# Two-stage attention and a squared-ReLU MLP on one core: batch 0 cut by head sets and token parts, hand-placed PSUM banks and a new step order

## The chip, the cores and the metric

The kernel runs on one core of a Trainium2 chip. The metric is device time in microseconds (us). Before the change it is 250.41 us, the median of 3 runs (250.41 to 251.27).

Engines are named as in the profile: PE (TensorE matmuls) and PEld (its weight loads), DVE (VectorE), ACT (ScalarE), POOL (GpSimd, which here mostly issues the loads), SP (SyncE, which issues the stores and the DMA transposes). Every engine takes its own instructions in program order.

## The reference

```
q, k, v: 8 batches x 8 heads x 576 tokens x 64     p: 8 x 8 x 32 x 64
packed = softmax(p k^T / 8) v            # 32 packed rows per head
att    = softmax(q packed^T / 8) packed  # 576 rows per head, 64 wide
x      = att with the heads side by side # 4608 x 512
h = x @ w_in                             # 512 x 2048
g = s * relu(h)^2 + b
out = g @ w_out                          # 2048 x 512, float32
```

## The kernel before

The work goes batch by batch. The attention output x is never formed: the softmax weights of the second attention (aT, 256 packed rows by 576 tokens) multiply a product of the packed rows with w_in (pw), which gives h directly. In h, 128 of the 2048 hidden columns make one "m"; there are 16. The term b is added as b times the column sums of w_out (biasrep), and s when a result leaves PSUM (svec).

The order of all work is one list of words at the end of the kernel, run in sequence; each word emits the instructions of one step, and so sets the order within each engine. The letters are followed by batch and part numbers:

- **L..** loads on POOL's queue: Lk, Lq, Lv (batch, half of the heads), Lp and Lpall (p), Lwi and Lwo (quarters of w_in and w_out, 512 KB each as bf16), Lsb (s and b, on SP). The loads cast float32 to bf16.
- **T** (on_pe) turns k or q on PE and copies them out of PSUM, **D** does it by a DMA transpose for batches 2 to 7; **V** (order_v) re-orders v on DVE; **PD, PP, PA, PPA** double and turn p.
- **F** first scores and their exp, **P** the packed rows, **X** their transpose, **S** second scores and exp, **A** the softmax sums: a matmul with ones, Ln and Exp of the negative on ACT, and a product on DVE (**G** in batch 0) that gives aT.
- **W** (packed_w) multiplies packed rows with w_in. It works in 64x32 tiles of the PE, eight of them at a time, two quarters of 512 columns in one word (one in batch 0), and is evicted by ACT and DVE.
- **M** (mlp_in) is one m: four matmuls of 288 columns into a tile of two PSUM banks, a relu on ACT (on DVE for a few of batch 0), a square on DVE into gT. **h** (mlp_in_half) does it for two m and one half of the tokens, in batch 0.
- **O**b.t**x**n are n of the 16 matmuls of 512 columns that give output tile t of batch b; with the last of them DVE scales and adds the bias into ysb and SP stores it.
- **BT** sums the columns of w_out (it needs all of w_out); **BC** makes the sum equal on all partitions by two float32 matmuls.
- **Z** and **Y** are matmuls on a tile of zeros that nobody reads (zps, or the next hps tile).

PSUM has 8 banks: pool psh has two tiles of two banks (hps), pool psy four tiles of one bank, and a step waits until a tile of its pool is free. Of the loaded k, q and v there is one buffer each.

Of the kernel before, what the change touches and what calls it, by code (L numbers as in the profile page):

```python
# [14 lines left out]
def kernel(  # L15
# [32 lines left out]
    JJ = NP // 16  # L48

# [8 lines left out]
    psh = ctx.enter_context(tc.tile_pool(name="psh", bufs=2, space=bass.MemoryType.PSUM))  # L58
    psy = ctx.enter_context(tc.tile_pool(name="psy", bufs=4, space=bass.MemoryType.PSUM))
# [17 lines left out]
    early = []  # L77

    def big(dt=F32):
        if early:  # L80
            return early.pop()
        return psh.tile([P, 2, NB if dt == F32 else 2 * NB], dt, tag="h", name="hps")
# [12 lines left out]
    pn = [constp.tile([P, 2, 2, D], BF16, name=f"pn{i}") for i in range(2)]  # L95
    pall = constp.tile([16 * (B - 2), 16, 2, D], BF16, name="pall")
# [10 lines left out]
    rowsf = constp.tile([P, P], F32, name="rowsf")  # L107
# [7 lines left out]
    def load(what, b, h0=0, h1=H):  # L115
        src = {"k": k, "q": q, "v": v}[what]
        if h0 == 0:
            raw[what, b] = rawp.tile([R, H, NC * D], BF16, tag=what + "n", name=what + "n")
        pool.dma_start(
            out=raw[what, b][:, h0:h1, :],  # L120
            in_=src[b, h0:h1].rearrange("h (r c) d -> r h (c d)", c=NC),
        )

# [21 lines left out]
    def load_sb():  # L145
        sp.dma_start(out=svec[:], in_=moe_s[0:1].unsqueeze(0).to_broadcast([P, 1]))
        sp.dma_start(out=bvec[:], in_=moe_b[0:1].unsqueeze(0).to_broadcast([P, 1]))
# [6 lines left out]

    def prep_p(b):
        pt = big(BF16)
        for x in range(2):
            tr(
                pt[:, 0, x * P:(x + 1) * P],
                pn[b][:, x, :, :],  # L160
                identb[:],
            )
        for c2 in range(2):
            act.copy(
                out=pbd[D * c2:D * c2 + D, :, b, :, c2, :],
                in_=pt[D * c2:D * c2 + D, 0, 0:2 * P].rearrange("p (g a j) -> p a g j", g=4, a=2),
            )

    def prep_pall():
        n = 16 * (B - 2)  # L170
        pts = [psy.tile([P, 8 * P], BF16, tag="y", name="pps") for _ in range(2)]
# [6 lines left out]
        for x in range(2):  # L178
            src = pts[x][:].rearrange("p (t n) -> p t n", n=P)[:, :, 0:n].rearrange(
# [9 lines left out]
    def on_pe(b, what, half):  # L189
        dst = (kT if what == "k" else qT)[b % 2]  # L190
        if what == "q":
            dst = dst[:].rearrange("p h c r -> p (h c r)")
        tpw = big(BF16)
        tp = [tpw[:, 0], tpw[:, 1]]
        split = b == 0 and what == "q"
        if split:
            tp[1] = psy.tile([P, 2 * NB], BF16, tag="y", name="tps")
        for h4 in range(4):
            for cp in range(CP):
                o = (h4 % 2) * HS + cp * R  # L200
                tr(
                    tp[h4 // 2][:, o:o + R],
                    raw[what, b][:, 4 * half + h4, cp * P:(cp + 1) * P],
                    identb[0:R, 0:R],
                )
        d = dst[:, half * 4 * HS:(half + 1) * 4 * HS].rearrange("p (a s) -> p a s", a=2)
        if split:
            act.copy(out=d[:, 0], in_=tp[0][:, 0:2 * HS])
            vec.tensor_copy(out=d[:, 1], in_=tp[1][:, 0:2 * HS])
        else:  # L210
            vec.tensor_copy(out=d, in_=tpw[:, :, 0:2 * HS])
# [8 lines left out]
    def order_v(b, h0=0, h1=H):  # L220
        vec.tensor_copy(
            out=vr[:, :, h0:h1, 0:D].rearrange("r c h d -> r h c d"),
            in_=raw["v", b][:, h0:h1, :].rearrange("r h (c d) -> r h c d", c=NC),
        )

    def first_scores(b, a):
        if a == 0:
            e1[b] = attp.tile([R, 2, NC, 4, NP], BF16, tag="e1", name="e1")
        s1 = big()
        for g in range(4):  # L230
            for cp in range(CP):
# [8 lines left out]
                )  # L240
        act.activation(
# [8 lines left out]
    def packed(b, half=None):  # L250

        if not half:
            pps[b] = psy.tile([P, NB], F32, tag="y", name="pps")
        pp = pps[b][:, 0:2 * DV].rearrange("p (a x) -> p a x", a=2)
        for a in range(2):
            for c in range(NC):
                for g in range(4) if half is None else (2 * half, 2 * half + 1):
# [8 lines left out]
        if half == 0:  # L266
            return
        rd = smp.tile([P, 2], F32, tag="rd", name="rd")
        vec.reciprocal(out=rd[:], in_=pp[:, :, D])
        pk[b] = smp.tile([P, 2, 2, D], BF16, tag="pk", name="pk")  # L270
        for a in range(2):
# [6 lines left out]
    def turned(b):  # L278

        pt = pps[b][:, NB // 2:].bitcast(BF16)  # L280
        for a in range(2):
            tr(pt[:, a * P:(a + 1) * P], pk[b][:, a].rearrange("p c d -> p (c d)"), identb[:])
        vec.tensor_copy(
            out=ppd[b % 2][:].rearrange("p a g j -> p (a g j)"),
            in_=pt[:, 0:2 * P],
        )

    def second_scores(b, by_half=False, with_w=False):
        e2[b] = attp.tile([P, 2, S], BF16, tag="e2", name="e2")
        tiles = [big() for _ in range(2)]  # L290
        for a in range(2):
            for g in range(4):
                for c2 in range(2):
                    t, i = (c2, a) if by_half else (a, c2)
                    mm(
                        tiles[t][NP * g:NP * g + NP, i, 0:HS],
# [6 lines left out]
        if by_half:  # L303
            exp_half(b, tiles, 0, 0)
            exp_half(b, tiles, 1, 0)
            s2[b] = tiles
            return
        if with_w:
            packed_w(b, [0])
        for a in range(2):  # L310
            act.activation(
# [6 lines left out]
    def exp_half(b, tiles, a, hf):  # L318
        act.activation(
            out=e2[b][:, a, hf * HS:(hf + 1) * HS],  # L320
            in_=tiles[hf][:, a, 0:HS],
            func=AF.Exp,
            scale=scale,
        )

    def weights_half(b, hf):
        if hf == 0:
            aT[b] = atp.tile([P, 2, S], BF16, tag="aT", name="aT")
        dps = big()
        for a in range(2):  # L330
            mm(dps[:, a, 0:HS], onesbd[:], e2[b][:, a, hf * HS:(hf + 1) * HS], start=True, stop=True)
        if hf == 0:
            exp_half(b, s2[b], 0, 1)
            exp_half(b, s2[b], 1, 1)
        ld = smp.tile([P, 2, HS], F32, tag="ld", name="ld")
        act.activation(out=ld[:], in_=dps[:, :, 0:HS], func=AF.Ln)
        rcd[hf] = smp.tile([P, 2, HS], F32, tag="rcd", name="rcd")
        act.activation(out=rcd[hf][:], in_=ld[:], func=AF.Exp, scale=-1.0)

    def weigh_half(b, hf):  # L340
        cols = slice(hf * HS, (hf + 1) * HS)
        vec.tensor_tensor(out=aT[b][:, :, cols], in0=e2[b][:, :, cols], in1=rcd[hf][:], op=ALU.mult)

    def weights(b, a):
        if a == 0:
            aT[b] = atp.tile([P, 2, S], BF16, tag="aT", name="aT")
        dps = big()
        for hf in range(2):
            mm(dps[:, hf, 0:HS], onesbd[:], e2[b][:, a, hf * HS:(hf + 1) * HS], start=True, stop=True)
        ld = smp.tile([P, 2, HS], F32, tag="ld", name="ld")  # L350
        act.activation(out=ld[:], in_=dps[:, :, 0:HS], func=AF.Ln)
        rc = smp.tile([P, S], F32, tag="rcd", name="rcd")
        act.activation(out=rc[:], in_=ld[:].rearrange("p a s -> p (a s)"), func=AF.Exp, scale=-1.0)
        vec.tensor_tensor(out=aT[b][:, a, :], in0=e2[b][:, a, :], in1=rc[:], op=ALU.mult)

    def packed_w(b, chs):
        if b not in pw:
            pw[b] = atp.tile([P, 2, DFF], BF16, tag="pw", name="pw")
        where = {}
        if len(chs) > 1:  # L360
            pair = [big() for _ in range(2)]
            where = {(a, x): pair[a][:, x, :] for a in range(2) for x in range(2)}
        if len(chs) != 2:
            single = [psy.tile([P, NB], F32, tag="y", name="wps") for _ in range(2)]
            where.update({(a, len(chs) - 1): single[a][:] for a in range(2)})
        for x, ch in enumerate(chs):
            for g in range(4):
                for a in range(2):
                    mm(
                        where[a, x][NP * g:NP * g + NP],  # L370
                        ppd[b % 2][D * a:D * a + D, a, g, :],
                        w_in_sb[D * a:D * a + D, g, ch * NB:(ch + 1) * NB],
                        start=True,
                        stop=True,
                        tile_position=(D * a, NP * g),
                    )
        if len(chs) > 1:
            for a in range(2):
                dst = pw[b][:, a, chs[0] * NB:(chs[0] + 2) * NB].rearrange("p (i f) -> p i f", f=NB)
                evict(dst, pair[a][:], a == 0)  # L380
        if len(chs) != 2:
            ch = chs[-1]
            if b == 0 and ch == 0:
                s2["w"] = single
                first_w(b, 0)
                return
            for a in range(2):
                evict(pw[b][:, a, ch * NB:(ch + 1) * NB], single[a][:], a == 0)

    def first_w(b, half):  # L390

# [329 lines left out]
```

The softmax here doesn't subtract the row's maximum and nothing guards it: scores larger than these inputs give would overflow.

## Time and profile before

| | |
|---|---|
| median of the runs | 250.41 us |
| span of the profiled execution, first to last instruction | 248.0 us |
| time of the profiled execution as a whole | not listed; the median is 2.41 us over the span |
| PE, DVE, ACT, POOL busy | 241.6, 144.4, 140.6, 29.1 us |
| mean granted TensorE clock | 1.000 |
| loads | 18.61 MB on POOL's queue, as counted at their destination |

The span is the time from the first to the last instruction. Busy times count an instruction from its start to its end; a matmul's end is modelled and overlaps the start of the next one. A mean of a group is the duration of one instruction; several back to back take less than the sum of the means.

### The profile page before, as it was taken

The numbers are of one execution on the slowest core, as the hardware profiler recorded it, in microseconds if no ns is written. First come the engines' busy times: TensorE is split into PE (matmuls) and PEld (weight loads), VectorE is DVE, ScalarE is ACT, GpSimd is POOL, SyncE is SP. The second block draws the span as 40 slices with busy tenths as digits, with TensorE's granted clock in tenths as the row PEclk, the third lists the DMA queues.
The fourth block names the chain that finished last, engine by engine and source line by source line (L and its number), as shares of the span: only waits on it lengthen the run. The fifth ranks groups of instructions, "written<-read, shape, count | busy, mean of one in ns | idle before, by whom it ended". The sixth has DMA issues, their size and how long they took to land.

```text
span 248.0 us, 5518 instructions
## 1 busy us (share of the span) xinstructions
PE 241.6 (97%) x2302; PEld 134.2 (54%) x2302; DVE 144.4 (58%) x278; ACT 140.6 (57%) x218; POOL 29.1 (12%) x43
## 2 busy tenths in 40 slices
PE   8999899999999999999999999999999999999994
PEld 2655565356644665456544654466545654366453
DVE  4438875599564864386538753586348742767221
ACT  2266742558837772758555953888266844578000
POOL 8733212000300012000300030000200000000000
PEclk9999999999999999999999999999999999999999
DMA  6999999999696589939798999337998811121133
GB/s 74 174 206 208 201 203 204 197 204 162 136 213 140 140 138 144 225 89 193 115 209 169 160 147 226 85 80 156 146 230 133 185 37 50 42 46 42 42 87 86
DMA packets 59450, 35.50 MB, mean 143 GB/s; under 512 B 32160, under 2 KB 54944, under 8 KB 59424
## 3 DMA queue, kind: packets, MB, share of 16 engines
q0 software_dynamic: 25184, 18.61, 50.8%
q1 hardware_dynamic: 34192, 16.49, 30.2%
q8 instruction: 18, 0.29, 0.5%
q14 instruction: 8, 0.07, 0.1%
q10 hardware_dynamic: 48, 0.03, 0.0%
HBM read 37.23 MB, written 9.44 MB: 188 GB/s over the span
## 4 chain that ended last, share of the span: by engine, by line
PE 82%; DMA 16%; issue 1%; POOL 0%; DVE 0%; POOLq 0%
PE yps L62 49%; PE hps L62 31%; DMA w_out_sb<-in_moe_w_out_dram 14%; DMA kn<-in_k_dram 2%; PE pps L62 1%; PE pps L65 1%; POOL kn L73 0%; DVE ysb L73 0%; POOL identb L73 0%; POOLq L73 0%; POOLq L705 0%
## 5 line engine op out<-in xcount | busy, mean ns | idle before, releaser
L62 PE MATMUL yps<-w_out_sb,gT 128*128 128x512 bf16 (+1 forms) x592 | 147.8, 374 | 0.6 <-DMA w_out_sb<-in_moe_w_out_dram 0.6
L73 ACT ACTIVATE rlu<-hps 128x576 bf16<-128x576 f32 x124 | 77.0, 649 | 23.1 <-PE hps L62 19.9
L62 PEld LDWEIGHTS <-gT 128*128 128x128 bf16 x592 | 54.8, 98 | 50.9 <-issue 8.8
L62 PE MATMUL hps<-aT,pw 128*128 128x288 bf16 x512 | 78.3, 285 | 0.2 <-ACT rlu L73 0.2
L73 DVE TENSOR_TENSOR gT<-rlu 128x576 bf16<-128x576 bf16 x128 | 57.8, 457 | 26.1 <-ACT rlu L73 23.3
L62 PEld LDWEIGHTS <-pw 128*128 128x128 bf16 x512 | 49.7, 97 | 26.3 <-issue 1.2
L73 DVE SCALAR_TENSOR_TENSOR ysb<-yps,svec,biasrep 128x512 f32<-128x512 f32 (+1 forms) x37 | 27.0, 733 | 21.7 <-PE yps L62 21.5
L73 ACT ACTIVATE e<-hps 96x768 bf16<-96x768 f32 (+2 forms) x34 | 21.8, 693 | 30.8 <-PE hps L62 30.6
L73 ACT CAST pw<-hps 128x1024 bf16<-128x1024 f32 x14 | 14.2, 1012 | 21.6 <-PE hps L62 21.0
L73 DVE TENSOR_TENSOR aT<-e,rcd 128x576 bf16<-128x576 bf16 x16 | 12.1, 757 | 23.4 <-ACT rcd L73 23.2
L73 POOL DMA_DIRECT2D kn<-in_k_dram x9 | 6.9, 767 | 130.1 <-DMA kT<-kn 97.8
L73 DVE CAST pw<-hps 128x1024 bf16<-128x1024 f32 x14 | 17.1, 1220 | 4.7 <-PE hps L62 4.6
L62 PE MATMUL zps<-zb 128*128 128x512 bf16 x42 | 13.6, 452 | 1.2 <-DVE zb L73 1.2
L73 ACT ACTIVATE rcd<-ld 128x576 f32<-128x576 f32 x16 | 10.9, 683 | 0.5
L73 ACT ACTIVATE ld<-hps 128x576 f32<-128x576 f32 x16 | 10.3, 643 | 1.2 <-PE hps L62 0.4
L62 PEld LDWEIGHTS <-ppd 64*32 64x32 bf16 x384 | 3.8, 88 | 11.0 <-issue 8.1
L62 PEld LDWEIGHTS <-zb 128*128 128x128 bf16 x56 | 5.6, 108 | 7.2 <-issue 3.2
L73 DVE RECIPROCAL rd<-pps 128x2 f32<-128x2 f32 x8 | 1.4, 171 | 13.3 <-PE pps L62 13.3
L62 PE MATMUL hps<-w_in_sb,ppd 64*32 64x512 bf16 x224 | 8.9, 381 | 0.0
L62 PEld LDWEIGHTS <-kT 128*128 128x128 bf16 x192 | 6.9, 98 | 2.5 <-issue 0.5
L73 DVE COPY vr<-vn 96x3072 bf16<-96x3072 bf16 (+1 forms) x9 | 8.0, 893 | 0.1
L73 POOL DMA_DIRECT2D vn<-in_v_dram x9 | 6.7, 751 | 5.5 <-DVE vr L73 2.9
(58 smaller groups left out, 104.0 us busy)
## 6 DMA issues: line engine op xcount, KB each, us to landing
out_dram<-ysb SPq DMA_DIRECT2D x23, 192.0 KB, 2.6
kn<-in_k_dram POOLq DMA_DIRECT2D x7, 576.0 KB, 7.1
vn<-in_v_dram POOLq DMA_DIRECT2D x7, 576.0 KB, 10.7
qn<-in_q_dram POOLq DMA_DIRECT2D x7, 576.0 KB, 13.3
out_dram<-ysb SPq DMA_DIRECT2D x24, 128.0 KB, 2.4
w_in_sb<-in_moe_w_in_dram POOLq DMA_DIRECT2D x4, 512.0 KB, 14.3
w_out_sb<-in_moe_w_out_dram POOLq DMA_DIRECT2D x4, 512.0 KB, 18.7
out_dram<-ysb SPq DMA_DIRECT2D x23, 64.0 KB, 2.1
```

Of the source, the lines that this page charges most:

```text
L62: return tc.keep_in_program_order(nc.tensor.matmul(*a, **kw))
L65: return tc.keep_in_program_order(nc.tensor.transpose(*a, **kw))
L73: return lambda *a, **kw: tc.keep_in_program_order(f(*a, **kw))
```

## The change

The change rewrites batch 0, the use of PSUM, and the list of words.

1. **Batch 0.** k and v load by head sets (even heads, then odd), q by token parts (chunks 0 to 3 of each row group, then 4 and 5: runs of 512 and 256 bytes at the destination in place of 768). First scores, packed rows and their transpose run per head set (F0.a, P0.a, X0.a); second scores, exp, sums, Ln, Exp and product run per token part and head set (S0.u.a, e, d, l, i, G); h works on two m and one token part (384 or 192 columns a matmul). W of batch 0 comes in 8 words of 256 columns.
2. **p of batch 0** is loaded first, by SP, as float32 into p0f, and cast on DVE; s and b load on POOL after w_out.
3. **PSUM** is one tile of 8 banks; each word names its banks after an @, and `take` hands them out. One word's later instructions (eviction, exp, square) are emitted when the word comes again, with a or v for ACT or DVE.
4. **W** of batches 1 to 7 is four words of 512 columns with a two-bank tile each, in place of two words of 1024.
5. **Bias.** BC is gone: DVE adds the four 32-partition groups of BT's result and writes biasrep with four multiplies.
6. **Loads.** k of batch 1 goes ahead of w_in, then w_in 1536:2048 and 512:1024, 0:256, v and q of batch 1, the rest of w_in, then w_out with p of batches 2 to 7 after its first quarter. In batches 2 to 5 some loads of one batch stand ahead of those of the batch before (Lk4 ahead of Lk3).
7. **Order.** The list of words is new throughout. It has 29 matmuls on zeros in place of 44 (12 more stand ahead of the list in both). Several output tiles are open at a time, and their last step (Q) is a word of its own.

The diff, cut to its core:

```diff
-    psh = ctx.enter_context(tc.tile_pool(name="psh", bufs=2, space=bass.MemoryType.PSUM))
-    psy = ctx.enter_context(tc.tile_pool(name="psy", bufs=4, space=bass.MemoryType.PSUM))
+    psp = ctx.enter_context(tc.tile_pool(name="psp", bufs=1, space=bass.MemoryType.PSUM))
+    banks = psp.tile([P, 8, NB], F32, name="banks")
+    spots = []
+    def take(n, dt=F32):
+        x = spots.pop(0)
+        t = banks[:, x:x + n, :]
+        return t if dt == F32 else t.bitcast(dt)
...
+    def load_part(what, part):
+        if what == "q":
...
+            x = slice(PARTS[part][0] * P, PARTS[part][1] * P)
+            pool.dma_start(
+                out=raw["q", 0][:, :, x],
+                in_=q[0].rearrange("h (r c) d -> r h (c d)", c=NC)[:, :, x],
+            )
+            return
...
+    def load_p0():
+        sp.dma_start(out=p0f[:], in_=p[0].rearrange("(x g) j d -> (g j) x d", x=2))
...
+    def scores0(u, a):
+        cols, w = part(u)
...
+        for g in range(4):
+            for c2 in range(2):
+                mm(
+                    s2[u][NP * g:NP * g + NP, c2, a * w:(a + 1) * w],
+                    ppd[0][D * c2:D * c2 + D, a, g, :],
+                    qh[D * c2:D * c2 + D, head(a, g), cols],
...
+    def packed_w0(c0, c1):
...
+        t = take(2)
+        for g in range(4):
+            for a in range(2):
+                mm(
+                    t[NP * g:NP * g + NP, a, 0:n],
+                    ppd[0][D * a:D * a + D, a, g, :],
+                    w_in_sb[D * a:D * a + D, g, c0:c1],
...
+        for a in range(2):
+            to((yield), pw[0][:, a, c0:c1], t[:, a, 0:n])
...
+    def squared(out, h):
+        on = yield
...
+        if on == "v":
+            vec.tensor_scalar_max(out=rlu, in0=h, scalar1=0.0)
         else:
+            act.activation(out=rlu, in_=h, func=AF.Relu)
+        yield
...
+        vec.tensor_tensor(out=out, in0=rlu, in1=rlu, op=ALU.mult)
...
-    def bias_rows():
-        ps = big()
-        mm(ps[:, 0, :], rowsf[:], biasrep[:], start=True, stop=True)
-        vec.tensor_scalar_mul(out=biasrep[:], in0=ps[:, 0, :], scalar1=bvec[:])
+        vec.tensor_copy(out=bias4[:], in_=ps[0:NP, 0, :])
+        for g in range(1, 4):
+            vec.tensor_tensor(out=bias4[:], in0=bias4[:], in1=ps[NP * g:NP * g + NP, 0, :], op=ALU.add)
+        for g in range(4):
+            vec.tensor_scalar_mul(out=biasrep[NP * g:NP * g + NP], in0=bias4[:], scalar1=bvec[0:NP])
...
+        Lq0.1 PD0 PP0@1 PP0v Z4@0 Tk0.0@2 Tk0.0v Z2@0 Tk0.1@4 Tk0.1v Tk0.1v PP0a Tk0.0a F0.0@6 V0.0 F0.0
...
+        Z1@3 d0.0@4 Lwi6.8 PD1 PP1@2 PP1v d0.1 e1.1 d1.0@6 Lwi2.4 l0.0 l0.1 d1.1 Z4@3 Tk1.1@0 l1.1 PP1v
+        Tk1.1v i0.0 Tk1.0@2 Tk1.0v Tk1.0v Lwi0.1 i0.1 l1.0 i1.0 Tk1.1a Z1@6 F1.0@4 Lv1 F1.1@6 G0.1 G1.0
+        Lq1 G0.0 i1.1 W0.7@0 W0.7v W0.6@2 W0.7a h0.14.0@0 h0.14.0v W0.6a W0.6a h0.12.0@2 G1.1 F1.1
...
+        Z5@1 X1 h0.6.0a X1a h0.12.1 h0.0.0 Tq1.0@6 Tq1.0a Tq1.0a Tq1.1@4 W0.1@2 W1.3@0 Tq1.1v Tq1.1v
+        S1@6,4 Lwo0.4 W0.1v W0.1a h0.2.0@2 W1.3v S1 W1.3v Lpall S1 h0.2.1@6 h0.2.1a A1.0@0 A1.0 W0.5@4
+        h0.2.0v W0.5a W0.5v W0.4@6 W1.0@2 W0.4v W0.4v Lwo4.8 W1.0a W1.0v W1.1@0 W1.1a W1.1v h0.2.0
+        h0.2.1 h0.10.0@4 h0.10.0v W1.2@6 W1.2a Lwo8.12 PA W1.2a h0.8.0@2 h0.6.0 h0.8.0a h0.8.0 O0.0x1@0
+        O0.1x1@1 O0.0x2 A1.1@6 A1.1 A1.1 O0.0x1 h0.10.1@4 h0.10.1v PPA0@2,3 O0.3x4@6 A1.0 O0.2x1@7 A1.0
+        O0.2x2 A1.1 PPA0 PPA0 h0.8.1@4 O0.1x1 h0.8.1a h0.8.1 O0.3x3 O0.1x2 h0.10.0 Lwo12.16 Lsb O0.0x2
+        O0.1x2 M1.6@4 Lk2 M1.6v PPA0 O0.0x1 h0.10.1 M1.0@2 M1.0v Lq2 O0.2x1 O0.3x1 M1.8@4 M1.8v M1.8
+        O0.1x1 BT@2 M1.4@4 M1.0 O0.1x1 M1.6 M1.4a M1.4 Lv2 Dk2 O0.1x1 O0.2x1 O0.1x1 O0.3x2 O0.2x2
...
+        O6.3x2 O7.2x5 Q7.2 O6.3x3 O7.1x1 O6.3x1 O7.1x1 O6.3x1 O7.1x1 O6.3x1 O7.0x3 O6.3x3 Q7.0 O6.3x1
+        O7.1x1 Q6.3 O7.1x8 O7.4x4 Q7.1 O7.4x7 Q7.4
```

## The prediction

> **What bounds the kernel now.** First the page: which engine is full, and at what clock.
>
> ```profile
> span 248.0 us, 5518 instructions
> ...
> PE 241.6 (97%) x2302; PEld 134.2 (54%) x2302; DVE 144.4 (58%) x278; ACT 140.6 (57%) x218; POOL 29.1 (12%) x43
> ...
> PE   8999899999999999999999999999999999999994
> ...
> PEclk9999999999999999999999999999999999999999
> ```
>
> PE is full at full clock, so DVE and ACT at 58% should not matter, but an average hides the stages. The chain of work that ended last, in order of time, splits the span in two:
>
> ```profile
> 8.51 14.02 DMA w_out_sb<-in_moe_w_out_dram
> 22.81 19.50 DMA w_out_sb<-in_moe_w_out_dram
> 42.35 0.59 PE yps L62 x2
> ...
> 228.15 16.46 PE yps L62 x92
> ```
>
> Until 42.35 us the chain is the loads; from there it is PE, piece after piece, to the last matmul near 244.6, and 3.4 us of last eviction and store end it. In the first part PE is "busy" because it is given work that nobody reads. The groups by shape:
>
> ```profile
> L62 PE MATMUL zps<-zb 128*128 128x512 bf16 x42 | 13.6, 452 | 1.2 <-DVE zb L73 1.2
> L62 PE MATMUL hps<-zb 128*128 128x512 bf16 x14 | 3.7, 379 | 0.0
> ```
>
> So only two things count: how much useful PE work is done when the loads stop being the limit, and what is left after it. As marker I take BT, the column sums of w_out, since it needs the last piece of w_out in both versions. The timeline around it, and single rows that I price with:
>
> ```profile
> 18.05 0.41 PE L62 MATMUL wps<-w_in_sb,ppd 64*32 64x512 bf16 x8
> 20.37 0.65 PE L62 MATMUL hps<-aT,pw 128*128 128x288 bf16 x4
> ...
> 44.89 1.05 PE L62 MATMUL hps<-w_out_sb,onesb 128*32 128x512 bf16 x16
> 47.47 1.10 PE L62 MATMUL hps<-biasrep,rowsf 128*128 128x512 f32 x2
> 48.40 1.03 PE L62 MATMUL yps<-w_out_sb,gT 128*128 128x512 bf16 x4
> 49.36 0.67 PE L62 MATMUL hps<-w_in_sb,ppd 64*32 64x512 bf16 x16
> 49.96 1.47 PE L62 MATMUL yps<-w_out_sb,gT 128*128 128x512 bf16 x6
> 51.26 1.40 DVE L73 SCALAR_TENSOR_TENSOR ysb<-yps,svec,biasrep 128x512 f32<-128x512 f32 x2
> 55.45 1.19 ACT L73 ACTIVATE rlu<-hps 128x576 bf16<-128x576 f32 x2 [0.27 <-PE hps L62]
> ```
>
> BT starts at 44.89; 203.1 us follow. Two relus in 1.19 us (one alone 0.65) mean that back to back one costs 0.54; two evictions in 1.40 (one alone 0.747) mean 0.65 on DVE. I use a mean where an instruction has waited, and about 0.09 less where it follows another.
>
> **The loads in the new order.** Issue time plus time to landing puts w_in's first quarter at 17.95 and w_out's last at 44.4; 5344 KB lie between (at the destination), so 202 KB/us. The new queue carries 160 KB more ahead of w_out's end (p of batches 2 to 7, 192 KB, moves in front of it; p of batch 0, 32 KB, moves to SP). That lands w_out at 45.2, q of batch 1 (4768 KB in) at 30.3 and the last of w_in (5536 KB) at 34.1, where before it was 27.8.
>
> Does the q load by token parts slow the queue? Its second part is 768 runs of 256 bytes. Here are the two nearest loads of before, the last w_out (issued 25.32) and p of batches 2 to 7, in 1536 runs of 128 bytes (issued 28.09):
>
> ```profile
> w_out_sb<-in_moe_w_out_dram POOLq DMA_DIRECT2D x1, 512.0 KB, 19.1
> ...
> pall<-in_p_dram POOLq DMA_DIRECT2D x1, 192.0 KB, 17.6
> ```
>
> They land at 44.4 and 45.7: 1.3 us where its bytes at 202 KB/us take 0.95, so 0.35 us for 1536 short runs, and at most 0.2 for 768. The Trainium skill ("DMA: Bandwidth & Descriptors", Specifications) speaks against the change: below 512 bytes a transfer becomes a read-modify-write and misses line rate. Read as twice the time, an estimate, q's part would hold back all later loads by 0.95 us and the sum below would be 249.9 in place of 248.9. I take the row; the rule's value is inside the range.
>
> **Until BT.** p by SP costs nothing: SP is idle then, and its 0.20 us cast on DVE runs under the 12 zero matmuls; were it late, PP0 would stop PE ahead of the first k. s and b behind w_out are not needed before BT's multiply. The two head-set chains make P0.0 start while set 1 is being scored, but second scores still wait for q near 14.5 us; then ACT runs 12 exps, Lns and inverses of 384 and 192 columns (about 0.49 and 0.33 by the slope between 288 columns, 0.415, and 576, 0.648; 4.9 us of means against 4.3 before). With w_in's first piece at 20.8 and W0.7's eviction, the first h is near 21.9, against 20.37. Of this 1.5 us nothing reaches the end by itself: PE is short of loads until 34 anyhow. Without that cover it would cost 1.5.
>
> What fixes BT is DVE. BT takes bank 2 from M1.0, whose relu is on DVE behind all this, in word order from the copies of q of batch 1: 2 copies of 0.46; 4 casts of 256 columns at 0.42; 4 casts of w of batch 1 at 0.684; 2 relus of 768 columns at about 0.96, one of 384 at 0.53, 2 of 576 at 0.755; 4 squares of 768 at about 0.60, 3 of 384 at 0.32; 2 products at 0.757; PA 0.41; 4 copies of turned p at 0.549. Sum 16.8 us in 29 instructions, 14.2 if all follow closely (29 x 0.09 less). It begins after Tq1.1: q lands 30.3, transposes take 1.2, and the step ahead of them (X1) waits for v and for five zero matmuls, so 32.4. BT is then between 46.6 and 49.2; the queue never lacks work, so I take a value near the first, 47.3. PE's own sum from w_in's end to BT is 11.2 us (26 O of 0.216, 3 M of 0.49, h, W and A), which gives 45.3: it is DVE, not PE or w_out, that comes last. **+2.4 us.**
>
> **After BT.** What PE no longer has to do, or has to do more:
> - O: 32 done before BT in the old order, 26 in the new: 6 x 0.216 = +1.30.
> - M of batch 1: none before, 3 now: 3 x 0.49 = -1.47.
> - W of batch 1, two groups of 16: 49.36 to 49.96 is 0.60, with 0.10 of entry each: -1.40.
> - A1.1, 2 x 0.122: -0.25. PPA's 16 transposes, 0.68: -0.68.
> - BC: 47.47 to 48.40: -0.93. In its place DVE gets seven more operations (about 5 us with the copy) behind BT; it has 12.6 us of work in the 11.6 us of PE until F2, while PE waits only for relus, mostly ACT's. No cost taken; M1.2 and F2.1 are next in line if it lags.
> - A group of small tiles costs its stream (16 of 512 columns: 0.43) and about 0.25 around it (0.60 + 0.10 less 0.43). Batches 2 to 7 had P, S, W, W: 24 groups. Now W is four words, but some stand next to each other or to S: 3, 4, 2, 2, 2, 2 groups besides P, 21 in all: -0.75.
>
> Sum -4.2. Steady O, M, F, P, X are the same matmuls. The evictions of W become 8 of 512 columns in place of 4 of 1024 per batch: ACT 4 x 0.588 against 2 x 1.01, DVE 4 x 0.684 against 2 x 1.22, some 0.6 us more for both, hidden at 58% load. Loads issued out of batch order (k of 4 ahead of k of 3) keep POOL waiting for DMA transposes; by the old rows (3 us to move 576 KB, 5 to 6 for a transpose) k of 3 is turned some 10 us ahead of F3. At the end Q7.1's store stands before the last one on SP: +0.3.
>
> **Sum:** +2.4 - 4.2 + 0.3 = -1.5, span 246.5. The median is 2.41 over the span of the profile; I carry that over: **248.9 us**. A difference under 0.5% (1.25 us) can't be told from none.
>
> **Rivals.**
> - The loads bound the head (0.15): DVE gets ahead, for which speaks that it waited in the old head too (1.87 of 5 us busy in 40 to 45); BT at 45.4, sum -3.4: 247.0.
> - DVE takes full means and PE waits once more for banks (0.17): BT at 49.4, +0.6: 251.0. For it: each bank is given by hand, and a late relu stops PE although other banks are free.
> - Slower: runs of M (0.18). In batches 4 to 7 some 15 M stand together with only 3 or 4 O between, where the old list mostly had one O per M (0.70 us of PE against 0.65 of ACT). At 0.54 per relu three tiles of two banks hide it; at 0.65, 13 relus take 8.5 us and PE, with 7.7 us of work, loses about 0.8 per batch, 4.8 in six: 253.7. It decides above 0.46 per batch. The pair of 1.19 us speaks against it.
> - The slots don't do what they say (0.05): if waits were kept for the one PSUM tile as a whole, every step would wait for every eviction, tens of us. Against it: w_in_sb is one tile too, and its first matmuls ran at 18.05 with its last quarter still loading.
> - Clock: the skill's "TensorE: Matmul & The Clock Gate" (Terms and Part 1) halves the clock after an idle window of about 3.4 us; the row shows full clock throughout, with zero matmuls filling. The new head has 15 fewer and, by my sum, pauses of about 1 us. By the row 0; by the rule, if one pause fills a window, about 1.7 us (an estimate): 250.6. Inside the range.
>
> The forecast itself has 0.45, and its own range is 247.6 to 250.2. **Chances:** faster by over 0.5%: 0.33 of the forecast and 0.15 of the loads, 0.48; within: 0.12 and 0.12 of full means, 0.24; slower: 0.05, 0.18, 0.05, so 0.28. The range 246.4 to 252.6 leaves out the low end of the loads' case, the upper half of the runs of M and the whole-tile case.
>
> **What would show it.** BT's matmuls (w_out_sb, onesb) near 47.3, with DVE over 90% busy from 33 to 47; first hps<-aT,pw near 22; no float32 matmul; from BT to PE's last matmul 195.5 us. If that stretch is over 197, runs of M or evictions stop PE: look for "PE hps <- ACT rlu" in the waits. If BT is near 45.4, DVE was not the limit; past 50 the head lost more than the rest saves.

## The result and the profile after

The changed kernel takes 250.19 us (median of 20 executions, 249.12 to 253.17), the kernel before 250.57 (20 executions, 250.35 to 251.34): a ratio of 0.9991 [0.997, 1.0012], no difference that can be measured. Forecast was 248.9. Executions of one kernel mostly agree within a microsecond or two, but some kernels, this one among them (253.17), also have executions that end 3 to 9 us later, which the ratios leave out and which are named where they matter.

The page of the profiled execution (which took 249.54 us), in the rows that were shown of before:

```profile
span 247.8 us, 5628 instructions
...
PE 235.5 (95%) x2299; PEld 133.9 (54%) x2333; DVE 160.7 (65%) x326; ACT 125.6 (51%) x223; POOL 31.8 (13%) x45
...
PE   8998999998999998999999999999999999999993
...
PEclk9999999999999999999999999999999999999999
```

PE is busy 6.1 us less (241.6 before), and the span is 0.2 us shorter: work went, the time did not. Most of it was work that nobody reads: the groups by shape show one group on zeros, with 4.6 us less in it than the two before (37 of its 41 matmuls are on record):

```profile
L62 PE MATMUL banks<-zb 128*128 128x512 bf16 x37 | 12.7, 463 | 1.6 <-DVE zb L73 1.2 <-issue 0.3
```

PE's timeline: the first h, BT, the three places after BT where PE stands still (in brackets the idle time before the instruction and what ended it), and the last matmuls:

```profile
21.32 1.47 PE L62 MATMUL banks<-aT,pw 128*128 128x384 bf16 x8 [0.44 <-DVE pw L73]
...
46.45 1.05 PE L62 MATMUL banks<-w_out_sb,onesb 128*32 128x512 bf16 x16
...
59.66 0.81 PE L62 MATMUL banks<-w_out_sb,gT 128*128 128x512 bf16 x2 [0.55 <-DVE ysb L73]
60.97 0.65 PE L62 MATMUL banks<-aT,pw 128*128 128x288 bf16 x4 [0.51 <-DVE ysb L73]
...
99.55 0.44 PE L62 MATMUL banks<-qT,ppd 64*32 64x288 bf16 x16 [0.95 <-DMA qT<-qn]
...
235.75 8.27 PE L62 MATMUL banks<-w_out_sb,gT 128*128 128x512 bf16 x42
```

BT is 1.56 us later than before (44.89), PE's last matmul ends at 244.02, so 197.6 us follow BT against 199.7 before, and the end takes 3.8 us against 3.4. +1.6, -2.1 and +0.4 (rounded) are the -0.2 of the spans. The three pauses are 2.0 us. The chain of waits names the same places; two of its pieces are no PE work:

```profile
46.45 5.16 PE banks L62 x38
...
58.86 2.07 DVE ysb L73 x3
...
93.08 6.43 DMA qT<-qn
```

What stands behind them, first DVE's timeline, then that of SP's queue:

```profile
56.26 0.96 DVE L73 COPY vr<-vn 96x3072 bf16<-96x3072 bf16 x1 [1.78 <-DMA vn<-in_v_dram]
...
58.86 2.06 DVE L73 SCALAR_TENSOR_TENSOR ysb<-banks,svec,biasrep 128x512 f32<-128x512 f32 x3
```

```profile
89.43 3.55 SPq L73 DMA_DIRECT2D out_dram<-ysb  x6
93.08 3.19 SPq L73 DMA_TRANSPOSE qT<-qn  x1
```

V2 waits 1.78 us for v of batch 2 and stands ahead of the last steps of three output tiles on DVE; their banks come free late, twice half a microsecond. Before the change V2 did not wait (DVE's timeline of before):

```profile
53.70 0.95 DVE L73 COPY vr<-vn 96x3072 bf16<-96x3072 bf16 x1
```

The list changed the loads under it: v of batch 2 is now issued behind q (38.17 and 36.93) and lands at 56.27; before, it was issued ahead of q (38.76 and 40.89) and landed at 51.5. And the transpose of q of batch 3 (Dq3) is issued behind six stores, at 93.08 where it was at 83.07 before; it lands 6.4 us later, and S3 waits for it.

### The profile page after: what moved, and what is told of

Its sections match the earlier page's. It is cut to its first block, busy times and chain, and to the rows that moved or that the text cites. A ratio compares the mean times of both kernels' runs of the same rounds, so it can differ in the third digit from the quotient of the medians.

```text
span 247.8 us, 5628 instructions
## 1 busy us (share of the span) xinstructions
PE 235.5 (95%) x2299; PEld 133.9 (54%) x2333; DVE 160.7 (65%) x326; ACT 125.6 (51%) x223; POOL 31.8 (13%) x45
## 4 chain that ended last, share of the span: by engine, by line
PE 82%; DVE 8%; ACT 3%; DMA 3%; issue 3%; DVEq 0%; ACTq 0%
PE banks L62 80%; DMA qT<-qn 3%; PE banks L65 2%; DVE ysb L73 2%; DVE rlu L73 2%; DVE gT L73 1%; DVE aT L73 1%; ACT rlu L73 1%; DVE pbd L73 1%; DVE kT L73 1%; ACT e L73 1%; DVE pw L73 1%; ACT rcd L73 1%; ACT pw L73 0%; ACT ld L73 0%
## 5 line engine op out<-in xcount | busy, mean ns | idle before, releaser
L62 PE MATMUL banks<-w_out_sb,gT 128*128 128x512 bf16 (+1 forms) x562 | 135.2, 373 | 2.7 <-issue 1.3
L73 ACT ACTIVATE rlu<-banks 128x576 bf16<-128x576 f32 (+2 forms) x102 | 60.8, 656 | 36.1 <-PE banks L62 32.8
L62 PE MATMUL banks<-aT,pw 128*128 128x288 bf16 (+2 forms) x512 | 74.0, 286 | 2.2 <-DVE pw L73 0.9
L73 DVE TENSOR_TENSOR gT<-rlu 128x576 bf16<-128x576 bf16 (+2 forms) x128 | 56.0, 455 | 9.9 <-ACT rlu L73 5.5
L73 DVE SCALAR_TENSOR_TENSOR ysb<-banks,svec,biasrep 128x512 f32<-128x512 f32 (+1 forms) x37 | 26.7, 733 | 37.5 <-PE banks L62 37.3
L73 ACT ACTIVATE e<-banks 96x768 bf16<-96x768 f32 (+3 forms) x34 | 21.8, 694 | 41.6 <-PE banks L62 41.6
L73 DVE CAST pw<-banks 128x512 bf16<-128x512 f32 (+1 forms) x40 | 23.5, 618 | 6.6 <-PE banks L62 6.6
L73 DVE TENSOR_SCALAR rlu<-banks 128x576 bf16<-128x576 f32 (+2 forms) x26 | 19.6, 761 | 6.0 <-PE banks L62 5.1
L73 ACT CAST pw<-banks 128x512 bf16<-128x512 f32 (+1 forms) x32 | 15.8, 556 | 1.9 <-PE banks L62 1.9
L62 PE MATMUL banks<-zb 128*128 128x512 bf16 x37 | 12.7, 463 | 1.6 <-DVE zb L73 1.2
```

Of the source, the lines that this page charges most:

```text
L62: return tc.keep_in_program_order(nc.tensor.matmul(*a, **kw))
L73: return lambda *a, **kw: tc.keep_in_program_order(f(*a, **kw))
```

## The experiments

The theory: the work taken off PE is gone, as forecast, and it comes back as the three waits, since words moved in the list were moved on DVE and SP too. The rivals: BT is late because of DVE, and that is where the time is; the new bias work on DVE holds later evictions. The first four kernels take the suspects one by one, then together. All ratios are to the kernel before, with the 95% interval; the changed kernel's is 0.9991 [0.997, 1.0012].

**V2 behind Q0.0.**

```diff
-O0.1x2 V2 O0.0x1 M1.7@4 ... Q0.1 Q0.0 O0.3x3
+O0.1x2 O0.0x1 M1.7@4 ... Q0.1 Q0.0 V2 O0.3x3
```

> One word moved: V2 (re-order of v of batch 2 on DVE) from ahead of M1.7 to behind Q0.0. Theory: the two PE waits for ysb at 59.7 and 61.0 us (0.55 + 0.51) come from DVE standing 1.8 us in front of V2 for v's load, so without it both waits are gone: 1.0 us less than the changed kernel, ratio to before about 0.995. Rival (the seven added bias operations on DVE hold the three Q's): both waits stay to over half, time as the changed kernel (0.999).

The ratio is 0.9979 [0.9956, 1.0003], not told apart from the changed kernel's. Both waits for ysb are gone, but S3 now waits 2.51 us for q of batch 3: PE came there 0.9 us earlier, and the transpose, issued at 92.18, took 8.0 us and landed 0.65 us later. Seven of twelve executions ended at 253.0 to 255.2 us, with a mean clock of .986 to .993. A wait was only pushed on.

**Dq3 right behind Dk4.**

```diff
-M2.6v Dk4 M2.8a ... Q1.2 Dq3 M2.12
+M2.6v Dk4 Dq3 M2.8a ... Q1.2 M2.12
```

> One word moved: Dq3 (DMA transpose of q of batch 3) from behind Q1.2 to behind Dk4, so SP issues it ahead of the stores of batch 1. Theory: the 0.95 us that PE waits at S3 is SP's order; it goes, 0.9 us less than the changed kernel, ratio about 0.9955. Rival (the transpose is slow because the DMA engines are busy, or S3's wait only shows another wait behind it): at most 0.3 us gained, ratio 0.998 to 0.999; below nothing if k of batch 3 is now turned later.

The ratio is 0.9947 [0.9931, 0.9963], 0.44% below the changed kernel: 1.1 us for one DMA instruction moved ahead of stores. In the profiled execution, one of the longer ones (251.10; the median is 249.24), S3 no longer waits, and F3 waits 1.01 us for k of batch 3, next in line. Three of 22 executions ended at 252.6 to 257.1.

**Three relus of batch 1 on ACT.**

```diff
-M1.6v ... M1.0v ... M1.8v
+M1.6a ... M1.0a ... M1.8a
```

> M1.6, M1.0 and M1.8 get their relu on ACT in place of DVE. Theory: DVE alone sets when BT starts (46.45), ACT is idle 5.6 us there, and the last of w_out has landed at 45.2; BT starts near 45.5, 0.9 us earlier, ratio about 0.9955. Rival (BT waits for w_out or PE's own work): BT stays within 0.2 us of 46.4, ratio 0.999.

The ratio is 0.9971 [0.9955, 0.9987], whose interval overlaps the changed kernel's. BT is at 46.39, hardly earlier than 46.45. PE's timeline ahead of it, where each piece begins as the one before ends:

```profile
43.97 1.36 PE L62 MATMUL banks<-aT,pw 128*128 128x288 bf16 x8
45.16 0.59 PE L62 MATMUL banks<-w_out_sb,gT 128*128 128x512 bf16 x2
45.59 0.65 PE L62 MATMUL banks<-aT,pw 128*128 128x288 bf16 x4
46.08 0.38 PE L62 MATMUL banks<-w_out_sb,gT 128*128 128x512 bf16 x1
46.39 1.05 PE L62 MATMUL banks<-w_out_sb,onesb 128*32 128x512 bf16 x16
```

With DVE relieved PE is full right up to BT. So DVE was not what alone fixed BT; PE's own work ends at nearly the same time, as the rival had it.

**All three.**

```diff
+ V2 behind Q0.0, Dq3 behind Dk4, M1.6a M1.0a M1.8a
```

> The three edits together. If the three waits are separate pieces of one PE chain they add: 1.0 + 0.9 + 0.9 = 2.8 us less than the changed kernel, ratio to before about 0.988. If they cover one another (an earlier BT only runs into v, q and k loads that land at the same time as before), 1.0 to 1.5 us, ratio 0.993 to 0.995.

The ratio is 0.9903 [0.987, 0.9935], from 247.37, 247.94 and 248.97; the other four of seven ended at 255.2 to 256.3. The profile shows one of those. SP's queue and PE's timeline:

```profile
87.28 6.86 SPq L73 DMA_TRANSPOSE kT<-kn  x1
```

```profile
99.00 1.46 PE L62 MATMUL banks<-pbd,kT 128*128 128x64 bf16 x24 [5.73 <-DMA kT<-kn]
```

The transpose of k of batch 3 began between POOL's issues of v and q of batch 4 (86.79 and 87.55). It took 11.7 us to land, where the same one with V2 late alone, issued at 84.3 ahead of both, took 4.3. PE stood for 5.73 us, and the granted clock was 0.50 from 96 us, while PE still stood, to 102 us. Hence a second theory: a DMA transpose beside a load takes twice as long, and where PE needs it soon, a pause follows and half clock with it.

**k of 3 and k of 4 in batch order.**

```diff
-Lk4 ... Dk4 ... Lk3 ... Dk3
+Lk3 ... Dk3 ... Lk4 ... Dk4
```

> Words Lk3 and Lk4, and Dk3 and Dk4, change places: k of batch 3 is loaded and turned ahead of k of batch 4. Theory: F3 (at 94.0 us) stands at the end of a chain through one k buffer (load k4, turn it, load k3, turn it), which ends within a fraction of a us of F3 and runs later when loads share the DMA engines; this is what makes single executions of the changed kernel differ by 4 us and the edits e1 to e4 differ by more, with the TensorE clock halved after the pause. With the swap k of 3 is turned near 79: no execution waits at F3, the spread falls under 2 us, the median to 249.3, ratio 0.995. Rival (the spread comes from the start of the kernel, from the first loads): spread and median as the changed kernel, ratio 0.998 to 0.999.

The ratio is 0.9992 [0.997, 1.0014], with 4 of 14 executions at 252.5 to 254.5: the order of the k loads alone is worth nothing. S3 still waits 2.39 us, for Dq3 behind the stores.

**The same with Dq3 right behind Dk3.**

```diff
+ Lk3 ... Dk3 Dq3 ... Lk4 ... Dk4
```

> The swap of e5, and Dq3 right behind Dk3. Theory: both waits of batch 3 (k at F3, q at S3) are gone without setting one against the other as in e2: 1 us less than e5, median 248.4, ratio 0.9915, and no execution over 250. Rival (transposes that stand together slow the loads, and the wait moves to batch 4): time as e5.

The ratio is 0.9926 [0.9914, 0.9938], with 248.26 to 248.91 us in all five executions. F3 (93.97) and S3 (98.49) wait for no DMA; the waits for ysb are left.

**All four edits** (swap, Dq3, V2 behind Q0.0, relus on ACT).

```diff
+ Lk3 ... Dk3 Dq3 ... Lk4 ... Dk4; Q0.0 V2; M1.6a M1.0a M1.8a
```

> e6 with V2 behind Q0.0 (e1) and the three relus on ACT (e3). Theory: the two waits for ysb (1.0 us) go on top of e6, and 0.3 us at BT: median 247.2, ratio 0.987; BT to the last matmul near 195.6 us, which is what the prediction had for the stretch. Rival (the DVE waits cover a load): 0.3 us under e6.

The ratio is 0.9881 [0.9864, 0.9898], from 247.32 and 247.64; two more executions took 252.94 and 253.98. In the profile none of the three waits is left, and from BT (46.77) to the end of PE's last matmuls (242.14) it is 195.4 us:

```profile
235.81 6.33 PE L62 MATMUL banks<-w_out_sb,gT 128*128 128x512 bf16 x34
```

**The same with the bias by two float32 matmuls,** as before the change.

```diff
-vec.tensor_copy(out=bias4[:], in_=ps[0:NP, 0, :])
...
+mm(t[:, 1, :], rowsf[:], biasrep[:], start=True, stop=True)
+vec.tensor_scalar_mul(out=biasrep[:], in0=t[:, 1, :], scalar1=bvec[:])
```

> e7 with the bias made equal on all partitions by two float32 matmuls again, as before the change, in place of seven DVE operations. If DVE's backlog behind BT costs nothing (as the prediction had it), this only puts 0.93 us back on PE: 0.9 us slower than e7. If the backlog costs PE something, 0 to 0.5 us slower, or faster than e7.

The ratio is 0.9917 [0.9904, 0.993]; one of five executions ended at 253.54. PE's timeline of this kernel, and then of the one with all four edits, from BT to F2:

```profile
46.71 1.05 PE L62 MATMUL banks<-w_out_sb,onesb 128*32 128x512 bf16 x16
...
52.13 1.02 PE L62 MATMUL banks<-biasrep,rowsf 128*128 128x512 f32 x2
...
59.45 0.86 PE L62 MATMUL banks<-pbd,kT 128*128 128x64 bf16 x24
```

```profile
46.77 1.05 PE L62 MATMUL banks<-w_out_sb,onesb 128*32 128x512 bf16 x16
...
58.47 0.86 PE L62 MATMUL banks<-pbd,kT 128*128 128x64 bf16 x24
```

From BT to F2 it is 12.74 us against 11.70: the two matmuls cost their 1.0 us in full, and the seven DVE operations in their place cost PE nothing. That rival falls.

**Where V3 stands.** V3 frees the buffer of v, so it decides when POOL issues v of batch 4. Three kernels move it: behind Q1.0 in the kernel with all four edits,

```diff
-M2.7a V3 O2.0x1@2 ... Q1.0 Lv4
+M2.7a O2.0x1@2 ... Q1.0 V3 Lv4
```

> The kernel with all four edits (k swap, Dq3 early, V2 behind Q0.0, three relus on ACT) had executions near 247.5 and others at 253 to 254 with a mean clock of .983 to .993. Theory: the late ones begin where the v and q loads of batch 4, released by V3, share the queues with the DMA transposes of batches 3 and 4, which then take 12 us in place of 5. Here V3 stands one word later, behind Q1.0 and directly ahead of Lv4, so that Lv4 is issued near 90.5 in place of 86.8, behind the issue of Dk4. Expected: no execution over 250, median near 247.5, a ratio of .988. Rival: where V3 stands does not matter, the late executions come from elsewhere, and about half of the executions stay at 253 to 254.

ahead of M2.3 in the kernel with the swap and Dq3 early,

```diff
-M2.3@2 M2.3a ... M2.7a V3 O2.0x1@2
+V3 M2.3@2 M2.3a ... M2.7a O2.0x1@2
```

> The kernel with the k swap and Dq3 early (248.3 to 248.9) with V3 moved ahead of M2.3, near 79 us, so that the v load of batch 4 is issued right behind k of batch 4, ahead of the transposes of batch 4 on SP. Theory: the transposes then always run beside these loads, land late, and hold SP's queue and PE at the scores of batch 3 or 4: nearly every execution at 252 or more, with a clock below .995. Rival: loads and transposes side by side are harmless, and it measures 248.3 to 248.9 as before.

and behind Q1.0 in the changed kernel, with nothing else.

```diff
-M2.7a V3 O2.0x1@2 ... Q1.0 Lv4
+M2.7a O2.0x1@2 ... Q1.0 V3 Lv4
```

> The changed kernel with the one word V3 moved behind Q1.0. Theory: its executions of 251 to 253 vanish, the wait of 0.95 us for q of batch 3 at S3 and the two of 0.5 us for evictions stay, so about 249.5 with a narrow spread and a ratio of .995 to .996. Rival: nothing changes, 249.1 to 253.2 with a median near 250.2.

The first has a ratio of 0.9932 [0.9912, 0.9952] and none of six executions over 249.42, but a median of 248.91, with a new wait of 0.9 us for a gT behind V3 on DVE. The second has 0.9919 [0.9902, 0.9937], 248.21 to 249.21 us, not the 252 that was expected; k of batch 4 did take 9.7 us to turn, but nobody needs it before F4 at 122. The third was expected at 249.5 and took 254.5 to 257.0 in all six, 1.0193 [1.0162, 1.0224]. POOL's timeline and SP's of the third show what was overlooked, PE's what it costs:

```profile
89.95 0.77 POOL L73 DMA_DIRECT2D vn<-in_v_dram  x1 [11.11 <-DVE vr L73]
```

```profile
88.82 3.82 SPq L73 DMA_DIRECT2D out_dram<-ysb  x6
92.74 5.92 SPq L73 DMA_TRANSPOSE qT<-qn  x1
```

```profile
103.05 0.44 PE L62 MATMUL banks<-qT,ppd 64*32 64x288 bf16 x16 [4.19 <-DMA qT<-qn]
```

v of batch 4 now runs into the transpose of q of batch 3, which lands after 10.3 us in place of 6.4. The overlap goes with it: v lands 5.9 us after the transpose begins here, 0.7 us after in the changed kernel (6.4 us), 1.6 us after with V2 late (8.0 us). The windows after the pause (PEclk is the third figure from the right):

```profile
102.00:103.00 1.00, 0.00 (x0) 0.00 (x0) 0.00 (x0) 0.00 (x0) 0.00 (x0) 1.00 0.45 143
103.00:104.00 1.00, 0.95 (x25) 0.37 (x25) 0.17 (x1) 0.57 (x2) 0.44 (x1) 0.84 0.74 219
104.00:105.00 1.00, 1.00 (x4) 0.42 (x3) 1.00 (x2) 0.62 (x2) 1.00 (x2) 0.50 0.07 27
...
106.00:107.00 1.00, 1.00 (x4) 0.46 (x3) 0.00 (x1) 0.97 (x3) 0.00 (x0) 0.50 1.10 161
107.00:108.00 1.00, 1.00 (x5) 0.29 (x3) 0.76 (x1) 0.97 (x2) 0.00 (x0) 0.95 1.31 201
```

Missing to full clock are 0.16, three times 0.50 (105 to 106 reads 0.50 too) and 0.05, that is 1.7 us, on top of the 4.2. That is the price the prediction worked out from the Trainium skill, "TensorE: Matmul & The Clock Gate" (Part 1: half rate after an idle window of about 3.4 us), and this trace agrees: the pause is longer than that, and 1.7 us are lost.

**No zeros in the list** (the 29; the 12 ahead of it stay), in the kernel with all four edits and V3 late.

```diff
-PP0v Z4@0 Tk0.0@2 Tk0.0v Z2@0 Tk0.1@4 ...
+PP0v Tk0.0@2 Tk0.0v Tk0.1@4 ...
```

> The same as the kernel with all four edits and V3 late, but without the 29 matmuls on zeros in the list; the 12 ahead of the list stay. Theory: the zeros only fill pauses of about 1 us that PE has anyway, ahead of BT[...]: the same time within 0.3 us. Rival: without them one or two windows at half clock appear ahead of 45 us (PEclk in the page), and BT comes 1 to 2 us later: about 249.

It takes 250.81 us, a ratio of 1.0012 [1.0, 1.0024], against 248.91 with them: the zeros are worth 1.9 us. The theory is wrong, and the loss is larger than its rival had it. Five windows from the head of the profiled execution, one of the longer ones (251.68):

```profile
10.00:11.00 1.00, 0.37 (x24) 0.24 (x24) 0.17 (x2) 1.00 (x2) 1.00 (x2) 1.00 1.37 181
11.00:12.00 1.00, 0.23 (x1) 0.10 (x1) 0.92 (x3) 0.33 (x2) 1.00 (x2) 1.00 1.52 187
12.00:13.00 1.00, 0.37 (x24) 0.30 (x24) 0.33 (x2) 0.08 (x1) 1.00 (x2) 1.00 1.87 180
13.00:14.00 1.00, 0.75 (x10) 0.76 (x11) 0.19 (x1) 0.27 (x1) 0.04 (x1) 0.60 1.44 200
14.00:15.00 1.00, 1.00 (x16) 1.00 (x14) 0.15 (x1) 0.79 (x1) 0.00 (x0) 0.50 1.30 202
```

The clock stays at 0.50 until 20 us. No pause in these windows was over 0.75 us; PE was merely busy 0.97 of the first 3 us. So the clock fell without the idle window named above; here the measurement decides. The other executions lost more clock: the mean is .963 to .984, and the profiled one has the highest. After the head, BT came 0.6 us later (46.70 against 46.11, no more than two executions of the kernel with all four edits differ: 46.77 and 46.12), F2 waits 1.1 us for k of batch 2, and an eviction comes 2.1 us late because DVE stands 2.1 us in front of the next V for its load. Together they are about the 3.7 us between the two profiled executions (247.98 with zeros); how the 1.9 us between the medians divides, and why the loads come later, was not isolated.

**What the last three settle.** In the kernel that took 255 us only Dq3 is moved:

```diff
-M2.6v Dk4 M2.8a ... Q1.0 V3 Lv4 ... Q1.2 Dq3 M2.12
+M2.6v Dk4 Dq3 M2.8a ... Q1.0 V3 Lv4 ... Q1.2 M2.12
```

> The changed kernel with V3 behind Q1.0, as in the run of 254.5 to 257.0, and only Dq3 moved right behind Dk4, so that q of batch 3 is transposed near 76 us with no load beside it. Theory: V3's place costs nothing by itself; what took 4.2 us, and 1.7 us more at half clock, was the transpose of q of batch 3 (10.3 us to landing beside the v load). Expected 248.0 to 249.5, no wait for qT at S3. Rival: V3 late holds its own buffer or bank chain: it stays at 253 or more.

The ratio is 0.9961 [0.9945, 0.9977], with 248.97 to 250.81 us in 13 executions. SP's queue shows the transpose in its new place, PE's timeline S3 without a wait:

```profile
75.71 3.08 SPq L73 DMA_TRANSPOSE qT<-qn  x1
```

```profile
99.18 0.44 PE L62 MATMUL banks<-qT,ppd 64*32 64x288 bf16 x16
```

Five microseconds hang on whether one transpose meets one load.

The kernel with all four edits once more:

```diff
+ Lk3 ... Dk3 Dq3 ... Lk4 ... Dk4; Q0.0 V2; M1.6a M1.0a M1.8a
```

> The kernel with all four edits once more, to see a late execution in the profile. Executions near 247.4 or at 253 to 254, about half of each. If the profiled one is late, theory: PE waits over 3.4 us in one place, behind a transpose of over 6 us on SP (k of batch 4 from 84.8), and the clock is 0.5 after it. Rival: the clock drops with no wait ahead of it.

Its two executions took 247.47 and, profiled, 253.99 us. The profiled one on POOL, SP, DVE and PE:

```profile
80.98 0.77 POOL L73 DMA_DIRECT2D kn<-in_k_dram  x1 [16.71 <-DMA kT<-kn]
86.76 0.77 POOL L73 DMA_DIRECT2D vn<-in_v_dram  x1 [5.01 <-DVE vr L73]
```

```profile
87.00 6.71 SPq L73 DMA_TRANSPOSE kT<-kn  x1
93.82 21.20 SPq L73 DMA_DIRECT2D out_dram<-ysb  x14
```

```profile
101.14 0.75 DVE L73 SCALAR_TENSOR_TENSOR ysb<-banks,svec,biasrep 128x512 f32<-128x512 f32 x1 [3.67 <-DMA out_dram<-ysb]
```

```profile
101.94 1.44 PE L62 MATMUL banks<-w_out_sb,gT 128*128 128x512 bf16 x3 [3.70 <-DVE ysb L73]
```

Read from the first line: k of batch 4 is issued at 80.98 (78.43 in the undisturbed execution), so its transpose starts at 87.00 in place of 84.77, beside v and not ahead of it. It lands after 11.9 us (4.4). The stores stand behind it until 93.82 (88.58), DVE finds no free ysb, PE no free bank, for 3.7 us; the clock is 0.50 from 101 to 107 us, and 2.7 us of that loss fall on work. The lateness is older than this meeting: the transpose of k of batch 2 begins at 50.50 (49.52), and F2 already waits 0.75 us for it. Where that first microsecond comes from stays open.

And V3 early with all four edits:

```diff
+ Q0.0 V2; M1.6a M1.0a M1.8a; Dk3 Dq3 ... V3 M2.3@2 ... Lk4 ... Dk4
```

> All four edits, and V3 ahead of M2.3, so that the v load of batch 4 is issued near 80 us. With two of the edits this place of V3 gave 248.2 to 249.2 and no late execution: k of batch 4, whose transpose then takes over 7 us, is not needed before F4 near 122. Theory: what matters is only whether a transpose that runs beside a load is one that PE needs soon; the two waits for evictions of 0.5 us go as well: 247.3 to 248.0, none over 250. Rival: the late executions of the kernel with all four edits come with V2 behind Q0.0: some at 252 to 254 remain.

The ratio is 0.9886 [0.9868, 0.9905], with 247.66 to 248.23 us in all four executions, none late. v and q of batch 4 are issued at 80.26 and 82.51. The transpose of k of batch 4 runs beside them and takes 9.4 us, which nobody needs; the stores behind it start at 92.54 and land in 3.6 us (median up to 102 us), against 6.1 in the execution of 253.99. PE's waits between 50 and 130 us, all of them:

```profile
PE banks L62 <- DVE vr L73: 0.2, 1, 0.2
```

All four executions are below both kernels, by 2.8 us against the one before and 2.4 us against the changed one. That none of four is late is weak evidence by itself: with V3 in its old place three of six were.

## Why the prediction was wrong

- **Landings and first h: right.** The last w_out was issued at 27.3 and landed 17.9 later, at 45.2, as worked out; the first h was at 21.3 (21.9). The 256-byte runs of q did not slow the queue.
- **BT at 47.3: near in place (46.45), half right in cause.** DVE was busy 11.19 of the 11.45 us before BT, as foretold, but PE was busy 11.13 of them, and with the three relus off DVE PE was full right up to BT. PE's own sum, which gave 45.3, was about 1 us short. The term is +1.56 in place of +2.4.
- **-4.2 after BT: right as work, and this is shown.** With the waits taken away the stretch is 195.4 us in two kernels; 195.5 was forecast. BC's 0.93 measured 1.0; with three fewer tile groups of 0.25 from F4 to F7, that stretch (80.78 us against 81.52) is 0.74 shorter, 0.75 by the sum. The other terms were not measured singly.
- **"No cost taken" for waits behind BT: the step that failed.** Two terms were put at nothing. The first is DVE's backlog until F2, "while PE waits only for relus": the seven new operations did cost nothing, but V2's 1.78 us of standing for v was not counted, and DVE meets V2 ahead of three last steps; that is 1.06 us. The second is the loads out of batch order. "k of 3 is turned some 10 us ahead of F3" was about 5.5 us (issued 84.23, landed near 88.5 by the 4.3 us that the same transpose took with V2 late, F3 at 94.0), which cost nothing here; but nothing was said of q of batch 3, whose transpose is moved behind six stores on SP: 0.95 us. Costed at nothing, the two are 2.0 us; with BT 0.85 earlier than forecast, which by luck hides part of it, and the rest in rounding, this is the 1.3 us between span 246.5 and 247.8. The prediction's own sign for it came true: the stretch after BT is over 197, at 197.6. The 2.41 us from span to median carried over (2.39), although in two parts: every execution takes some 1.75 us more than its span, and the profiled ones of both kernels are some 0.65 us shorter than their medians (249.54 against 250.19; before, 248.0 + 1.75 against 250.41).
- **Rivals.** Runs of M: PE waits 0.2 us for a relu, so that case is dead (its 4.8 us counts six batches where its reading names four, which would be 3.2). The loads as the bound: w_out lands 1.25 us before BT. The whole-tile wait: none seen. The clock: full in the profiled execution, as taken; but 4 of the 20 have a mean of .991 to .993 and took 251.8 to 253.2 us. That those come from the same meeting of Dq3 and the v load is argued from the kernel with V3 late, not seen in a profile. The kernel before has such executions too: 10 of 44 measured beside the first experiments have a mean of .993 and took 251.2 to 251.3 us, so the low clock alone is no mark of the change.

## What to carry to other kernels

A word moved in a list moves on every queue that its step uses: for each load, transpose and copy ask what stands ahead of it, what behind, and when the consumer comes. Give a DMA transpose that is needed soon a stretch with no load beside it, and put the loads beside one that is not. A saving on the full engine is real only if the next thing it waits for has slack of that size. Here one wait taken away often only lengthened the next; with all of them gone the forecast saving appeared.

## What was not expected of the hardware

- In batches 3 and 4 a transpose of 576 KB of k or q by SP took 4.3 to 8.5 us to land, and 9.4 to 11.9 us in five profiles where v of batch 4, or v and q, had been issued up to 5 us before it (the three edits, all four in the late execution, V3 late alone, and V3 early twice); its own time on SP's queue was 2.3 to 4.0 us in the one case and 5.9 to 7.2 in the other.
- Not every load does this: k of batch 4 in the changed kernel was turned at 72.69, while v of batch 3 landed until 75.6, and took 5.1 us. What in the meeting costs the time stays open.
- The clock went to 0.50 around pauses of 3.7 to 5.7 us, in two profiles while PE still stood, and also after 3 us in which PE was busy for a third, with no pause over 0.75 us. The work behind the pause of 4.2 us lost 1.7 us, that behind the pause of 3.7 us lost 2.7.
